# Interleaving two products, splitting the attend and moving fill pieces in a recurrent-memory step

## The chip, the cores and the metric

The kernel runs on one core of one Trainium2 chip. The metric is device time in microseconds (us) of one execution. Several executions of each kernel are taken, those of a comparison on one chip in the same rounds. The record marks every run quoted here as of the fast state; their mean granted TensorE clock is 0.971 to 0.995. A ratio of two kernels is the mean time of one kernel's fast runs over that of the other's of the same rounds, so it is not quite the ratio of the medians that are quoted beside it.

## The reference, cut to what matters

The output is a gated mix of two branches. Branch B is an ordinary gated feed-forward layer and the change does not touch it. Branch A is a recurrence: 64 segments of 32 rows are done one after the other, and 8 memory rows of a segment's output are fed into the next.

```python
mem = mem0
for s in range(n_seg):                              # 64 steps, each needs mem of the one before
    h = concat([mem, x[32*s : 32*s+32]])            # 40 rows, 1024 wide
    q, k, v = h @ Wq, h @ Wk, h @ Wv                # 32 heads of 128
    p = softmax(mask(q @ k.T * scale))
    o = (p @ v) @ Wo
    mem = o[:8]                                     # to the next step
    outs.append(o[8:])
```

## The kernel before: the parts that matter

A step works on two halves of the heads, r = 0 and r = 1. TensorE runs 64 products in a fixed order, the "walk". A q, k or v product is 4 matmuls of 512 columns that run side by side in the array; an o product is 8 matmuls of 256 columns.

```python
ORDER = (("k", 0), ("q", 0), ("v", 0), ("k", 1), ("q", 1), ("o", 0), ("v", 1), ("o", 1))
walk = [(m, r, i) for m, r in ORDER for i in seq(m, r)]      # 8 products each
```

I call the eight groups k0, q0, v0, k1, q1, o0, v1, o1. The weights do not all fit into SBUF. Twelve slots of 512 KB are "paired": k 0 and 2, q 0 and 2, v 0, 1, 2, 4, 6, o 0, 2, 4. Such a slot is used first for one half and must be refetched from HBM before the other half's product of the same number. In half 0 the paired products come first, in half 1 last, so that a refetch has the longest time.

```python
def spent(k):                    # after a product
    n = home[k]
    done[n] += 1
    if done[n] < len(uses[n]) and uses[n][done[n]] != k:
        fetch(n)                 # 512 KB, issued on the SP queue when TensorE is done with the slot
```

Beside its own products a step has "fill pieces" f1 and f2, eight each: products for the row blocks that do not depend on the recurrence (f2 is a q fill in 29 of the 64 steps and a v fill in 30). They are placed where TensorE would otherwise wait for another engine.

```python
on("v", 0, 4, lambda: trans(qT))
on("q", 1, 4, lambda: trans(kT))
...
on("o", 0, 0, some(f1, 4))              # 4 pieces, while tA, tB of half 0 are made
on("o", 0, 0, lambda: attend(ua))       # p @ v: 16 matmuls with tA, vA, then 4 with tB, vB
on("o", 0, 0, some(f1, 1)); trans(qT); some(f1)         # (shortened)
on("o", 0, 1, lambda: scores(1))
...
on("o", 1, 0, lambda: evac(bank_of["v", 1], vA))        # ScalarE copies v1 to vA
on("o", 1, 0, some(f2, 5))
on("o", 1, 0, lambda: attend(ub))
on("o", 1, 0, some(f2))                 # the other 3
on("o", 1, 1, lambda: fill_evac(...))
...
# end of the step:
act_copy(a_bf, PB[XO])                  # two halves
if k2 and k2[0] == "q":
    fill_trans()                        # 4 transposes, in the gap while ScalarE copies a_bf
transpose(a_bf); dve_copy(h_next)       # the recurrence goes on with k0 of the next step
```

Matmuls of the attend use the array in four row tiles (a profile shows 32*128), products in four column tiles (128*32), transposes the whole (128*128). And one detail of memory turns out to matter: `vA = al("vA", [128, 4, 128], at=oT.off)`, that is, vA lies in the memory of oT, which the o products read.

## Time and profile before

| | before |
|---|---|
| time, median of 3 (lowest to highest) | 2300.04 us (2299.81 to 2300.23) |
| one recurrent step, mean of 62 | 24.50 us |
| TensorE busy | 89% |
| refetched weights | 12 of 512 KB a step, 513 MB in q1 over the whole run, start-up and feed-forward included |

These are lines of the page of the kernel before: the span, TensorE (PE) busy time, two costly groups, and two DMA queues with packets, megabytes and the share of 16 DMA engines. A group line has source line, engine, operation, out<-in, count, busy us and mean ns, then idle us before it.

```profile
span 2304.5 us, 80168 instructions
PE 2060.9 (89%) x36594; PEld 1099.2 (48%) x36614; DVE 901.2 (39%) x2164; ACT 604.1 (26%) x1280; POOL 616.0 (27%) x1107
...
L670 PE MATMUL pb<-sl,hT 128*32 128x512 bf16 x12288 | 756.8, 383 | 43.2 <-DMA sl<-in_A_Wq_dram 18.4
...
L682 PE MATMUL pb<-sl,oT 128*32 128x256 bf16 x8192 | 281.8, 275 | 56.2 <-issue 46.1
...
q1 hardware_dynamic: 189536, 513.35, 61.7%
...
q8 instruction: 287, 4.70, 0.8%
```

What TensorE waits for in the recurrent part is in the waits view (matmuls only, 150 to 1690 us; who waited, for whom, total us, times, longest):

```profile
PE pb L682 <- issue: 46.1, 44, 2.3
PE pb L670 <- DMA sl<-in_A_Wq_dram: 18.4, 28, 1.6
...
PE pb L670 <- issue: 8.5, 12, 1.4
PE pb L670 <- DMA sl<-in_A_Wv_dram: 7.9, 13, 1.0
...
PE pb L682 <- DMA sl<-in_A_Wo_dram: 7.6, 14, 1.0
```

L682 are the o products, L670 the q, k and v products. "Issue" means that no semaphore ended the gap. Looked at one by one, these gaps end about 2.4 us (median of 81; half of them between 2.33 and 2.48) after a 16,384-byte packet of the instruction queue (q8) started, so I read them as TensorE having no instructions to run. The Trainium skill, "Runtime: NRT & Kernel Launch", Instruction fetch mechanics, says that instructions are refilled by DMA in 16 KiB blocks of 256 and calls the cost of crossing a block "mostly hidden". The block size agrees (287 packets, 4.70 MB); hidden it is not here.

The end of a step, from the timeline of TensorE (start, length, engine, line, operation; L697 are fill pieces, L641 and L646 the two parts of the attend, L588 transposes, L871 the transposes of a_bf):

```profile
1014.03 1.25 PE L697 MATMUL pb<-sl,hR 128*32 128x512 bf16 x20
1015.21 0.27 PE L641 MATMUL pb<-tA,vA 32*128 32x40 bf16 x16
1015.33 0.19 PE L646 MATMUL pb<-tB,vB 32*128 32x64 bf16 x4
1015.45 0.83 PE L697 MATMUL pb<-sl,hR 128*32 128x512 bf16 x12
...
1018.63 0.40 PE L588 MATMUL pb<-ident,tok 128*128 128x128 bf16 x4
1019.08 0.40 PE L871 MATMUL pb<-ident,a_bf 128*128 128x128 bf16 x2
1019.58 2.77 PE L670 MATMUL pb<-sl,hT 128*32 128x512 bf16 x48
```

The reader sees five pieces (x20), the attend in one go, three pieces (x12); at the end the q fill's transposes fill the gap before the a_bf transposes. In a step with a v fill nothing stands there, and TensorE is idle for some 0.4 us.

### The profile page before, as it was taken

Reading aid. Unit: us, or ns where it says so; the run is one execution under the profiler, and the core shown is the slowest. Engines: PE = TensorE matmul, PEld = TensorE weight load, DVE = VectorE, ACT = ScalarE, POOL = GpSimd, SP = SyncE. Lnnn points to the kernel's source line nnn. Section 1 sums busy time; section 2 is a strip of 40 time slices with the busy share of each in tenths; the row PEclk is TensorE's granted clock in tenths of the full one; section 3 lists DMA queues with packets and bytes.
Section 4 is the critical chain, followed back from the end, with each engine's and each line's share of the span. In section 5 each row is a group of like instructions: output and inputs, shape, how many; then the busy total and the mean of one; then the engine's idle time right before and its main releaser. Section 6 shows DMA issues by size and latency. Waiting matters only on the chain.

```text
span 2304.5 us, 80168 instructions
## 1 busy us (share of the span) xinstructions
PE 2060.9 (89%) x36594; PEld 1099.2 (48%) x36614; DVE 901.2 (39%) x2164; ACT 604.1 (26%) x1280; POOL 616.0 (27%) x1107
## 2 busy tenths in 40 slices
PE   2588998899999998898998998998879999999998
PEld 1244555555555555555555455554444444444443
DVE  3134333334334343343343433333335164363452
ACT  1122232222323222232232322222223032131230
POOL 5233333343333433333333333333210000000000
PEclk9999999999999999999999999999999999999999
DMA  9968788788788787787887887887782802606206
GB/s 358 379 213 305 257 304 294 261 289 309 265 303 302 272 316 271 269 322 265 290 323 248 302 302 256 302 303 266 270 330 90 276 34 80 230 1 208 103 1 237
DMA packets 225714, 576.45 MB, mean 250 GB/s; under 512 B 30424, under 2 KB 42584, under 8 KB 225376
## 3 DMA queue, kind: packets, MB, share of 16 engines
q1 hardware_dynamic: 189536, 513.35, 61.7%
q0 software_dynamic: 26624, 44.14, 5.6%
q10 hardware_dynamic: 9216, 13.83, 1.7%
q8 instruction: 287, 4.70, 0.8%
q14 instruction: 51, 0.42, 0.1%
HBM read 539.71 MB, written 31.39 MB: 248 GB/s over the span
## 4 chain that ended last, share of the span: by engine, by line
PE 65%; DMA 24%; issue 5%; DVE 3%; ACT 2%; POOL 1%; SPq 0%; ACTq 0%; POOLq 0%; DVEq 0%
PE pb L670 20%; PE pb L929 14%; DMA sl<-in_A_Wq_dram 11%; PE pb L682 9%; PE pb L697 6%; PE pb L966 6%; DMA sl<-in_A_Wo_dram 5%; PE pb L712 3%; PE pb L588 3%; DMA sl<-in_A_Wv_dram 3%; DMA wd<-in_B_w_down_dram 2%; PE pb L609 1%; DMA xr_scr<-xr 1%; PE pb L641 1%; PE pb L603 1%
## 5 line engine op out<-in xcount | busy, mean ns | idle before, releaser
L670 PE MATMUL pb<-sl,hT 128*32 128x512 bf16 x12288 | 756.8, 383 | 43.2 <-DMA sl<-in_A_Wq_dram 18.4
L670 PEld LDWEIGHTS pb<-sl,hT 128*32 128x32 bf16 x12288 | 331.7, 97 | 327.2 <-DMA sl<-in_A_Wq_dram 38.8
L682 PE MATMUL pb<-sl,oT 128*32 128x256 bf16 x8192 | 281.8, 275 | 56.2 <-issue 46.1
L576 ACT ACTIVATE tok<-pb 128x512 bf16<-128x512 f32 x320 | 191.0, 597 | 458.0 <-PE pb L670 393.0
L682 PEld LDWEIGHTS pb<-sl,oT 128*32 128x32 bf16 x8192 | 213.0, 97 | 98.7 <-issue 54.6
L697 PE MATMUL pb<-sl,hR 128*32 128x512 bf16 x3072 | 215.0, 390 | 19.6 <-DMA sl<-in_A_Wq_dram 7.3
L929 PE MATMUL pb<-xT,wg 128*128 128x512 bf16 x896 | 213.2, 381 | 16.2 <-DVE GT L945 8.4
L655 POOL COPY oRc<-oT 128x128 bf16<-128x128 bf16 x128 | 98.6, 770 | 452.4 <-DVE oT L579 445.4
L929 PE MATMUL pb<-xT,wu 128*128 128x512 bf16 x896 | 211.7, 379 | 0.0
L966 PE MATMUL pb<-wd,GT 128*128 128x512 bf16 x876 | 194.7, 379 | 8.9 <-DMA wd<-in_B_w_down_dram 7.7
L579 DVE CAST oT<-pb 128x160 bf16<-128x160 f32 x256 | 71.2, 320 | 230.4 <-PE pb L646 230.4
L937 ACT ACTIVATE s<-pb 128x512 f32<-128x512 f32 x112 | 66.8, 596 | 326.8 <-PE pb L929 307.3
L929 PEld LDWEIGHTS pb<-xT,wg 128*128 128x128 bf16 x896 | 87.1, 98 | 125.1 <-DVE GT L945 12.8
L576 ACT ACTIVATE vA<-pb 128x512 bf16<-128x512 f32 x128 | 76.4, 597 | 265.9 <-PE pb L670 265.9
L966 PEld LDWEIGHTS pb<-wd,GT 128*128 128x128 bf16 x896 | 86.4, 98 | 117.2 <-DMA wd<-in_B_w_down_dram 15.5
L588 PE MATMUL pb<-ident,tok 128*128 128x128 bf16 x1280 | 128.1, 222 | 13.2 <-ACT tok L576 8.9
L929 PEld LDWEIGHTS pb<-xT,wu 128*128 128x128 bf16 x896 | 87.7, 98 | 105.9 <-issue 0.3
L938 DVE SCALAR_TENSOR_TENSOR tp<-s,pb 128x512 f32<-128x512 f32 x112 | 76.9, 687 | 155.2 <-ACT s L937 155.1
L588 PEld LDWEIGHTS pb<-ident,tok 128*128 128x128 bf16 x1280 | 72.6, 98 | 123.2 <-ACT tok L576 94.3
L579 DVE COPY kT<-pb 128x512 bf16<-128x512 bf16 x128 | 51.9, 405 | 197.9 <-PE pb L588 197.9
L614 DVE TENSOR_REDUCE st<-pb 128x8 f32<-128x320 f32 x128 | 62.9, 492 | 159.6 <-PE pb L609 159.6
L697 PEld LDWEIGHTS pb<-sl,hR 128*32 128x32 bf16 x3072 | 83.3, 98 | 81.5 <-DMA sl<-in_A_Wq_dram 8.4
(76 smaller groups left out, 1929.7 us busy)
## 6 DMA issues: line engine op xcount, KB each, us to landing
sl<-in_A_Wv_dram SPq DMA_DIRECT2D x331, 512.0 KB, 9.9
sl<-in_A_Wo_dram SPq DMA_DIRECT2D x205, 512.0 KB, 5.9
sl<-in_A_Wk_dram SPq DMA_DIRECT2D x142, 512.0 KB, 5.5
sl<-in_A_Wq_dram SPq DMA_DIRECT2D x142, 512.0 KB, 7.4
wd<-in_B_w_down_dram SPq DMA_DIRECT2D x56, 1024.0 KB, 6.4
qk_scr<-stg POOLq DMA_DIRECT2D x64, 128.0 KB, 5.8
qkr<-qk_scr POOLq DMA_DIRECT2D x128, 64.0 KB, 5.4
wg<-in_B_w_gate_dram SPq DMA_DIRECT2D x3, 1792.0 KB, 13.2
```

The lines of the kernel that those rows point to most:

```text
L576: op("act", lambda e: e.activation(o, i, ACTF.Copy), rd=rd, wr=wr)
L579: op("dve", lambda e: e.tensor_copy(o, i), rd=rd, wr=wr)
L588: ins = e.transpose(PBV[TT][:, j * 128:(j + 1) * 128], tok[:, j * 128:(j + 1) * 128], ident[:, :])
L655: op("pool", lambda e: e.tensor_copy(oRc[:, u, :, :].rearrange("p c x -> p x c"), oT[:, :, :, 32:40].rearrange("p g j c -> p (g j) c")), r ...
L670: ins = e.matmul(PB[bk][32 * g:32 * g + 32, :], lhsT=h[:, i, :], rhs=w[:, g * 512:(g + 1) * 512], start=(p % 8 == 0), stop=(p % 8 == 7))
L682: ins = e.matmul(PB[XO][32 * g:32 * g + 32, 0:256], lhsT=oT[:, gp_, 2 * jj + hh, 0:32], rhs=w[:, c:c + 256], start=(r == 0 and p % 8 == 0 ...
L697: ins = e.matmul(PB[b][32 * g:32 * g + 32, :], lhsT=h[:, k[2], :], rhs=w[:, g * 512:(g + 1) * 512], start=(n == 0), stop=(n == 7))
L712: ins = e.matmul(PB[b][32 * g:32 * g + 32, 0:256], lhsT=t[:, :, 2 * i + hh], rhs=w[:, c:c + 256], start=(ends[0] and i == 0 and hh == 0), ...
L929: ins = e.matmul(PB[bk][:, 0:FB], lhsT=w[:, kc, cc:cc + 128], rhs=xT[:, :, :, kc, :].rearrange("p t i c -> p (t i) c"), start=(kc == 0), s ...
L937: op("act", lambda e, hg=hg: e.activation(s1[:, :], hg, ACTF.Square, scale=SQ), rd=[BK(bg)], wr=[s1.r()])
L938: op("dve", lambda e, hg=hg, t=t: e.scalar_tensor_tensor(out=t[:, :], in0=s1[:, :], scalar=1.0, in1=hg, op0=ALU.add, op1=ALU.mult), rd=[BK ...
L966: ins = e.matmul(PB[bank[2 * k + hf]][:, :], lhsT=GT[:, j, tb * 128:(tb + 1) * 128], rhs=w[:, jj, hf * 512:(hf + 1) * 512], start=(j == 0) ...
```

## The change

Its intent: finish v1 two products earlier, so that its copy to vA is ready sooner; let the main part of the attend go as soon as tA is there and the small tail with tB a little later; with fewer pieces needed before and after the attend, put the two pieces saved into the gap at the end of the step, for every kind of f2 fill. The transposes of a q fill, which stood in that gap, go into the next step's k0.

```diff
-        walk = [(m, r, i) for m, r in ORDER for i in seq(m, r)]
+        groups = [[(m, r, i, n) for n, i in enumerate(seq(m, r))] for m, r in ORDER]
+        walk = [x for g in groups[:5] for x in g] + [groups[5 + (c == "v")].pop(0) for c in "ooovvovvovvovvoo"] + groups[7]
 # ... in scores(): pA and tA are now made before pB and tB; E8 lies 128 bytes later, clear of tA ...
 # ... attend() is split: attend() has the 16 matmuls of tA and vA, attend_tail() the 4 of tB and vB ...
-            on("v", 0, 4, lambda: trans(qT))
+            on("v", 0, 5, lambda: trans(qT))
-            on("q", 1, 4, lambda: trans(kT))
+            on("q", 1, 5, lambda: trans(kT))
-            on("o", 0, 0, some(f1, 4))
+            on("o", 0, 0, some(f1, 2))
             on("o", 0, 0, lambda: attend(ua))
+            on("o", 0, 0, some(f1, 2))
+            on("o", 0, 0, lambda: attend_tail(ua))
-            on("o", 1, 0, some(f2, 5))
+            on("o", 1, 0, some(f2, 3))
             on("o", 1, 0, lambda: attend(ub))
-            on("o", 1, 0, some(f2))
-            if k2:
-                on("o", 1, 1, lambda: fill_evac(*k2, F2, stage[1]))
+            on("o", 1, 0, some(f2, 1))
+            on("o", 1, 0, lambda: attend_tail(ub))
+            on("o", 1, 0, some(f2, 2))
 # ... end of the step, after the copies to a_bf:
-            if k2 and k2[0] == "q":
-                fill_trans()
+            run(f2)                                   # the last two pieces
+            if k2:
+                fill_evac(*k2, F2, stage[1])
 # ... after the copies to h_next:
             if k2 and k2[0] == "q":
-                fill_put(stage[1], "dve")
+                pend.append(fill_trans)               # run at product 4 of the next k0
+                pend.append(lambda: fill_put(stage[1], "dve"))
```

## The prediction

> **What bounds the kernel.** TensorE is busy 89% of 2304.5 us (engine table). The change touches the 64 recurrent steps (about 120 to 1680 us), 24.5 us each by the transpose that starts a step (timeline). Of these I count, from starts of matmuls against the usual spacing of the same pair, 21.7 us of undisturbed issue and some 2.3 us of stalls:
> - About 1.2 us "issue": no semaphore ends these gaps. They end 2.2 to 2.5 us after a 16 KB packet of the instruction queue starts, so I read them as TensorE waiting for instructions. Some 0.9 us of it lies in o0 and early v1, where products of 8 matmuls of 256 columns use instructions fastest. The Trainium skill ("Runtime: NRT & Kernel Launch", Instruction fetch mechanics) has blocks of 256 instructions fetched by DMA, "mostly hidden"; the trace agrees on the block (287 packets of 16,384 bytes), not on "hidden".
> - About 0.8 us weight DMA (waits view, weight loads in the phase: Wq 38.8, Wv 17.1, Wo 13.1 us). The 12 refetches of a step land every 1.3 to 1.7 us from 5.6 to 22.6 us of the step; the last Wv lands at 18.15 (used at 18.98), the last Wo at 22.56 (used at 23.47). So a step can shrink by 0.5 to 0.7 us at most, some 40 us in all.
> - 650 ns from the last o matmul to the a_bf transpose, in steps without a waiting q fill.
>
> **What the change does, per step.**
> 1. Two fill pieces (217 ns each) into the 650 ns gap. In the 30 steps with a v fill this is free: -0.43 us. In the 30 with a q fill, the fill transposes sat there; they move into the next step's k0, where such a set costs 312 + 168 + 149 - 217 = 0.41 us: net zero, part hidden in the Wq wait.
> 2. Attend split: one more switch between row-tiled and column-tiled matmuls. Product to attend takes 312 ns against 217, attend to product 114; one more round costs 312 + 114 - 217 - 14 = 0.195 us, 0.39 us a step. ("TensorEngine Tiling (Array Packing)", Key Properties: mode switches drain the array; 312 against 217 agrees.)
> 3. Attend hardly waited for tA, tB or vA (matmul idle 7 us in all), so "waits on tA only" gains nothing itself; it lets pieces move. With two pieces instead of three after the o1 attend, the first o1 product waits about 0.13 us for oT.
> 4. Interleaving lowers the instruction rate: o0 used 16 instructions per 0.24 us, the mix 24 per 0.46. I guess 0.35 of the 0.9 us goes. But v1's last refetched pair is used 0.48 us earlier, against 0.8 us of median slack: Wv and Wo waits grow by 0.17.
> 5. Transposes one product later: the 311 ns before them is the drain, so nothing is gained.
>
> Sum: v steps -0.43 +0.39 +0.13 -0.35 +0.17 = -0.1 us; q steps up to +0.3, half absorbed. I add 5 us for chances of better instruction timing and predict **2291 us**, 2268 to 2314; faster by over 2%: 0.07, within 2%: 0.89, slower: 0.04.
>
> **Right if** fill matmuls fill the gap before the a_bf transpose; each attend shows two 312 ns entries; "issue" before Wo products falls by a third; waits for Wv rise; Wq waits fall after q fills; steps average 24.3 to 24.6 us.
>
> **Wrong if** the instruction stalls depend on where blocks of 256 fall (every reorder shifts them), which can swing 1 us a step; if Wv/Wo waits eat more than 0.2; or if fill stores, now 1.5 us later, ease or crowd the first refetches (the first takes 4.6 us, later ones land every 1.5).

## The result, and the profile after

| | before | after |
|---|---|---|
| median (lowest to highest), 4 runs each | 2300.14 us (2299.81 to 2310.69) | 2324.74 us (2322.47 to 2332.34) |
| ratio, 95% interval | | 1.0102 (1.0065 to 1.0138) |
| one recurrent step in the profiled run, mean of 62 | 24.50 us | 24.73 us |

The kernel became 1% slower, and the time lies outside the range predicted. The two profiled runs are 19.2 us apart (2304.5 and 2323.7); 14 us of that lie in 62 steps (62 times 0.226), the rest before and after.

The page and the waits of the kernel after (L690 are now the o products, L679 the q, k and v products):

```profile
span 2323.7 us, 80137 instructions
PE 2094.9 (90%) x36614; PEld 1095.0 (47%) x36614; DVE 914.4 (39%) x2164; ACT 604.9 (26%) x1280; POOL 613.7 (26%) x1107
...
PE pb L690 <- issue: 36.6, 38, 2.1
PE pb L679 <- DMA sl<-in_A_Wv_dram: 24.5, 33, 2.0
PE pb L679 <- issue: 11.0, 10, 2.5
PE pb L679 <- DMA sl<-in_A_Wq_dram: 10.9, 21, 1.1
```

Waits for instructions at the o products fell by 9.5 us (and rose by 2.5 at the others), those for Wq fell by 7.5, and those for Wv went from 7.9 to 24.5. The timeline of one step's second half shows all parts of the change (L705 fill pieces, L645 and L655 the two parts of the attend, L881 a_bf):

```profile
1003.65 0.40 PE L679 MATMUL pb<-sl,hT 128*32 128x512 bf16 x4
1004.95 0.40 PE L679 MATMUL pb<-sl,hT 128*32 128x512 bf16 x4 [0.90 <-DMA sl<-in_A_Wv_dram]
...
1006.06 0.82 PE L705 MATMUL pb<-sl,hR 128*32 128x512 bf16 x12
1006.94 0.27 PE L645 MATMUL pb<-tA,vA 32*128 32x40 bf16 x16
1007.14 0.40 PE L705 MATMUL pb<-sl,hR 128*32 128x512 bf16 x4
1007.47 0.21 PE L655 MATMUL pb<-tB,vB 32*128 32x64 bf16 x4
1007.61 0.61 PE L705 MATMUL pb<-sl,hR 128*32 128x512 bf16 x8
...
1009.84 0.61 PE L705 MATMUL pb<-sl,hR 128*32 128x512 bf16 x8
1010.40 0.40 PE L881 MATMUL pb<-ident,a_bf 128*128 128x128 bf16 x2
1010.90 1.05 PE L679 MATMUL pb<-sl,hT 128*32 128x512 bf16 x16
1011.88 0.40 PE L591 MATMUL pb<-ident,tok 128*128 128x128 bf16 x4
1012.21 2.13 PE L679 MATMUL pb<-sl,hT 128*32 128x512 bf16 x36
```

The last refetched v product waits 0.90 us for its weights. The tail starts 0.33 us after the single piece (a piece alone takes 0.217). Two pieces (x8) fill the gap before L881 as meant, and the q fill's transposes (L591) now interrupt k0, at 1011.88.

The second attend also waited for vA. Its copy should have started earlier than before; it did not. These are the groups of ScalarE's waits before its copies to vA, first of the kernel before, then of the kernel after:

```profile
ACT vA L576 <- PE pb L670: 265.9, 127, 5.8
```

```profile
ACT vA L579 <- PE pb L690: 101.2, 34, 4.8
ACT vA L579 <- PE pb L679: 99.1, 63, 1.6
```

Before, all copies waited for the v products. After, 34 of the 64 copies of v1 waited for the o products (L690): vA lies in the memory of oT, so the copy may not start before the last o product has read it, and that is now the last of the mixed group. In 28 steps ScalarE also had a stage copy to do just before, whose place (at o product 6) had moved behind most of v1:

```profile
1005.72 0.60 ACT L579 ACTIVATE stg<-pb 128x512 bf16<-128x512 bf16 x1 [2.92 <-PE pb L591]
1006.28 0.60 ACT L579 ACTIVATE vA<-pb 128x512 bf16<-128x512 f32 x1
```

The stage copy is not what held it: in all 62 steps looked at, with or without it, the copy to vA starts 36 to 53 ns after the last o0 product ended (before: 36 to 52 ns after the last v1 product). So the head start that v1's earlier end was to give did not exist. The second attend starts 54 to 57 ns after the copy's end in every one of these steps.

### The profile page after: what moved, and what is told of

Its sections match the earlier page's. It is cut to its first block, busy times and chain, and to the rows that moved or that the text cites. A ratio compares the mean times of both kernels' runs of the same rounds, so it can differ in the third digit from the quotient of the medians.

```text
span 2323.7 us, 80137 instructions
## 1 busy us (share of the span) xinstructions
PE 2094.9 (90%) x36614; PEld 1095.0 (47%) x36614; DVE 914.4 (39%) x2164; ACT 604.9 (26%) x1280; POOL 613.7 (26%) x1107
## 4 chain that ended last, share of the span: by engine, by line
PE 63%; DMA 27%; issue 4%; DVE 3%; ACT 2%; POOL 1%; SPq 0%; ACTq 0%; POOLq 0%; DVEq 0%
PE pb L679 19%; DMA sl<-in_A_Wv_dram 15%; PE pb L940 14%; PE pb L690 8%; PE pb L977 6%; DMA sl<-in_A_Wq_dram 6%; PE pb L705 5%; PE pb L591 3%; PE pb L720 3%; DMA wd<-in_B_w_down_dram 2%; ACT vA L579 1%; DMA sl<-in_A_Wo_dram 1%; DMA xr_scr<-xr 1%; PE pb L645 1%; PE pb L612 1%
## 5 line engine op out<-in xcount | busy, mean ns | idle before, releaser
L679 PE MATMUL pb<-sl,hT 128*32 128x512 bf16 x12288 | 797.4, 381 | 56.3 <-DMA sl<-in_A_Wv_dram 25.1
L679 PEld LDWEIGHTS pb<-sl,hT 128*32 128x32 bf16 x12288 | 327.0, 96 | 307.5 <-DMA sl<-in_A_Wv_dram 40.5
L690 PE MATMUL pb<-sl,oT 128*32 128x256 bf16 x8192 | 331.2, 275 | 40.7 <-issue 36.6
L690 PEld LDWEIGHTS pb<-sl,oT 128*32 128x32 bf16 x8192 | 222.4, 97 | 122.3 <-issue 47.7
L705 PE MATMUL pb<-sl,hR 128*32 128x512 bf16 x3072 | 243.6, 395 | 19.9 <-DMA sl<-in_A_Wq_dram 8.9
L591 PE MATMUL pb<-ident,tok 128*128 128x128 bf16 x1280 | 127.8, 223 | 9.9 <-ACT tok L579 6.5
L591 PEld LDWEIGHTS pb<-ident,tok 128*128 128x128 bf16 x1280 | 72.7, 98 | 128.4 <-ACT tok L579 96.2
L953 DVE SCALAR_TENSOR_TENSOR tp<-tp,pb 128x512 f32<-128x512 f32 x112 | 76.9, 687 | 78.7 <-ACT tp L952 78.7
## 6 DMA issues: line engine op xcount, KB each, us to landing
wg<-in_B_w_gate_dram SPq DMA_DIRECT2D x3, 1792.0 KB, 14.3
```

Of the source, the lines that this page charges most:

```text
L591: ins = e.transpose(PBV[TT][:, j * 128:(j + 1) * 128], tok[:, j * 128:(j + 1) * 128], ident[:, :])
L679: ins = e.matmul(PB[bk][32 * g:32 * g + 32, :], lhsT=h[:, i, :], rhs=w[:, g * 512:(g + 1) * 512], start=(n == 0), stop=(n == 7))
L690: ins = e.matmul(PB[XO][32 * g:32 * g + 32, 0:256], lhsT=oT[:, gp_, 2 * jj + hh, 0:32], rhs=w[:, c:c + 256], start=(r == 0 and n == 0 and ...
L705: ins = e.matmul(PB[b][32 * g:32 * g + 32, :], lhsT=h[:, k[2], :], rhs=w[:, g * 512:(g + 1) * 512], start=(n == 0), stop=(n == 7))
L953: op("dve", lambda e, hu=hu, t=t: e.scalar_tensor_tensor(out=t[:, :], in0=t[:, :], scalar=1.0, in1=hu, op0=ALU.add, op1=ALU.mult), rd=[BK( ...
```

## The experiments

Theory A: TensorE itself got more work per step (two more switches between row and column tiles, q transposes out of the gap into k0, a wait for vA) than the filled gap gives back, and interleaving gives nothing, since what it could save in waits for instructions it loses in waits for Wv. Rivals: B, the interleaving does save instruction stalls, as predicted, and something else costs more; C, the whole loss is waits for refetched weights; D, interleaving costs TensorE time itself; and, for single parts, that the switches or the moved transposes are hidden in waits.

To judge, I use the mean time of a step's sections, taken from the starts of matmuls in the profiled run (62 steps), and a tally of TensorE's gaps: every gap of over 380 ns between the starts of two successive matmuls in these steps, except before the a_bf transpose, less 217 ns, put down to what released it (217 ns is the usual spacing of two products); "instructions" are gaps that no semaphore ended, within 3.6 us after an instruction packet started. Totals are in us over 62 steps:

| kernel | instructions | Wq | Wv | Wo | vA |
|---|---|---|---|---|---|
| before | 70.8 | 24.6 | 10.7 | 8.1 | 3.5 |
| after | 60.3 | 16.2 | 30.4 | 1.1 | 15.4 |
| e1 interleaving alone | 67.0 | 14.1 | 28.7 | 1.7 | 3.1 |
| e3 end pieces, v steps | 75.4 | 20.5 | 9.6 | 11.5 | 3.5 |
| e4 end pieces, all steps | 83.3 | 15.5 | 5.5 | 17.6 | 3.5 |
| e7 after, not interleaved | 69.3 | 22.0 | 6.4 | 9.6 | 15.6 |
| e8 other order | 78.7 | 21.5 | 5.8 | 3.6 | 3.5 |
| f1 before, no refetches | 0 | 0 | 0 | 0 | 3.4 |
| f2 after, no refetches | 0 | 0 | 0 | 0 | 15.2 |

These are of one profiled run each; differences of a few us between rows mean little. The vA column overstates the rise: a piece and the attend after it start 312 ns apart even without a wait, so each new vA gap counts 95 ns too much. Against these 312 ns the second attend of the kernel after starts 0.10 us a step later than in the kernel before, 6 us in all.

### Parts of the change alone

All are made from the kernel before, with that part only.

**e1: interleaving.**

```diff
-        walk: o0 then v1        (oooooooovvvvvvvv)
+        walk: o0 and v1 mixed   (ooovvovvovvovvoo)
```

> The kernel before with only the o0/v1 interleaving (ooovvovvovvovvoo). Theory A (the interleaving costs, because v1's refetched pairs are used 0.5 us earlier while their landing does not move): waits for Wv rise by 0.3 us a step or more, instruction stalls fall by only 0.15, Wo waits fall by 0.1: 0 to +8 us against before. Rival B (the interleaving saves instruction stalls as the prediction had it, and the loss lies in the split of attend and in the moved transposes): -10 to -20 us.

Measured: 2303.88 us against 2299.24, ratio 1.0021 (0.9992 to 1.0049), about +5 us, not clear of noise (in the profiled run a step takes 24.50 us, as before). It fits theory A; the 10 to 20 us gain of B lies outside the interval. The waits of e1 (L684 o products, L673 q, k and v):

```profile
PE pb L684 <- issue: 43.2, 42, 2.6
PE pb L673 <- DMA sl<-in_A_Wv_dram: 24.9, 38, 1.7
...
PE pb L673 <- issue: 12.0, 10, 2.4
PE pb L673 <- DMA sl<-in_A_Wq_dram: 9.1, 21, 1.4
```

Issue of both kinds is 55.2 against 54.6 before: nothing saved. Wv went from 7.9 to 24.9, and part of that came back from Wq and Wo. In the tally, Wv and Wo together went from 18.8 to 30.4, 0.19 us a step.

**e2: attend split**, with one piece between main part and tail, the number of pieces in each half unchanged.

```diff
-            some(f1, 4); attend(ua); some(f1, 1)
+            some(f1, 3); attend(ua); some(f1, 1); attend_tail(ua); some(f1, 1)
-            some(f2, 5); attend(ub); some(f2)
+            some(f2, 4); attend(ub); some(f2, 1); attend_tail(ub); some(f2)
```

> The kernel before with only attend split into a main part and a tail with one fill piece between them (same number of pieces in each half). Theory A and the prediction's step 2: two more drains a step, 0.195 us each, so +0.39 us a step on TensorE; where the step then waits less for weights, part is hidden: +12 to +25 us. Rival (drains are hidden, the split is free): within 3 us of before.

Measured: 2311.22 us, ratio 1.0043 (1.0014 to 1.0071), about +10 us, a little under the range that theory A gave. The split is not free. How much of its cost hides is shown by f4 below.

**e3: end pieces in v steps only** (4 pieces, attend, 2, and 2 at the end), attend whole.

```diff
-            some(f2, 5); attend(ub); some(f2)
+            some(f2, 4); attend(ub); some(f2, 2 if k2 and k2[0] == "v" else 99)
+            run(f2)                      # after the copies to a_bf
+            if k2 and k2[0] == "v":
+                fill_evac(*k2, F2, stage[1])
```

> The kernel before with two of the v fill's pieces moved behind the last o product, only in the 30 steps with a v fill (pieces 4 + attend + 2, then 2 at the end). Both theories: the gap before the a_bf transpose is filled for free, -0.43 us in 30 steps and +0.06 for a wait on oT: -11 us; if the weight DMA sets the pace of a step, Wo and Wq waits take much of it back and it is -3 us or less.

Measured: 2296.84 us, ratio 0.9983 (0.9952 to 1.0015), about -4 us, not clear of noise. Less than the 11 us of theory A, and in the direction of the limit named there: waits for Wo rose from 8.1 to 11.5 us and those for instructions from 70.8 to 75.4.

**e4: end pieces in all steps**, q transposes in the next k0, attend whole: the end part of the change.

```diff
-            if k2 and k2[0] == "q":
-                fill_trans()
+            run(f2)
+            if k2:
+                fill_evac(*k2, F2, stage[1])
+            # q: fill_trans and fill_put appended to pend, run at product 4 of the next k0
```

> As e3, and also in the 30 steps with a q fill, whose transposes then move into the next step's k0 as in the change. Prediction's step 1: the q steps gain 0.43 and the next k0 loses 0.41, so no better than e3 (-8 to -11 us). Rival (the moved transposes hide in the wait for Wq): another -8 to -12 us beyond e3.

Measured: 2308.02 us, ratio 1.0036 (0.9998 to 1.0074), about +8 us, just not clear of noise, and outside what either theory gave: 12 us worse than e3. From the start of k0 to the scores, steps after a q fill take 6.63 us at the median against 6.18 before, about what was predicted for the transposes; but the gain in the q steps is not seen, and waits for Wo are 17.6 us against 8.1.

**e10: the q transposes moved into k0, and nothing put into the gap.**

```diff
-            if k2 and k2[0] == "q":
-                fill_trans()
-                fill_put(stage[1], "dve")
+                pend.append(fill_trans)
+                pend.append(lambda: fill_put(stage[1], "dve"))
```

> The kernel before with only the q fill's transposes moved from the end of the step into the next step's k0 (nothing put in their place). Theory A: the gap they leave stays about 650 ns, the k0 part of the following step grows by 0.41 us in 30 steps: +8 to +12 us. The prediction's 'half absorbed' by the wait for Wq: +3 to +6 us. If the Wq wait hides all of it: 0.

Measured: 2317.14 us against 2303.17, ratio 1.0056 (1.0018 to 1.0094), about +13 us. That is all of the 29 sets (0.44 us each in f2 below, 12.9 us; the prediction had 0.41); half of it hiding in the Wq wait, as predicted, is not seen in the time, though the Wq wait did fall to 14.3 us from 24.6 in the tally. The runs of this kernel spread from 2304.83 to 2331.75, so the size is good to a few us only.

The parts alone add up: e1 +5, e2 +10 and e4 +8 make +23 us; the change as a whole costs 24 us. Each part is good to some 7 to 9 us, so the close match is partly luck. Without refetches the same three parts give 0, +27 and -8 us (f3, f4 and f6 below).

### Undoing the interleaving

**e7: the kernel after with o0 and v1 in their old order.**

```diff
-        ... for c in "ooovvovvovvovvoo"]
+        ... for c in "oooooooovvvvvvvv"]
```

> The changed kernel with o0 and v1 in their old order, all else changed. From e1 (+5 us alone): undoing the interleaving gives back about 5 us, +17 to +20 us against before; but v1 then ends right before the second attend with only 3 fill pieces to cover the copy to vA, which costs up to 0.4 us a step, so +25 to +45 us if that wait is not hidden. Rival B (interleaving saves stalls): well over +24 us without any longer wait for vA.

Measured: 2329.01 us against 2304.06, ratio 1.0109 (1.0094 to 1.0124), about +25 us, the same as the change itself within the noise (1.0109 against 1.0102). Waits for Wv fell from 30.4 to 6.4 us, and those for instructions, Wq and Wo rose by 9.0, 5.8 and 8.5: they come in each other's place. (The mixed order has 9.0 us less of instruction waits here, more than the 3.8 in e1, and no shorter time.) The wait for vA is 15.6 us with the old order and 15.4 with the new one. So my expectation that the mixed order shortens that wait was wrong, and it agrees with what was read above: the copy to vA starts after the last of the 16 products of o0 and v1, which is an o0 product in the mixed order and a v1 product in the old one (here 37 to 52 ns after its end).

### The same mixing with the refetched pairs later

**e8: another mixed order.**

```diff
-        walk: o0 then v1        (oooooooovvvvvvvv)
+        walk: o0 and v1 mixed   (ooovovovovovovvv)
```

> The kernel before with o0 and v1 interleaved in another order (ooovovovovovovvv): the same mixing, but v1's last three refetched pairs stay in their old places. Theory A (the refetched pairs' earlier use is what made e1 lose): Wv waits back at 0.2 us a step, instruction stalls still 0.1 to 0.2 below before: -3 to -10 us, some 10 us better than e1. Rival D (the interleaving itself costs, wherever the pairs lie): no better than e1, +3 us or more.

Measured: 2300.12 us against 2304.06, ratio 0.9978 (0.9963 to 0.9992), about -5 us, a small gain that is clear of noise, and 10 us better than e1. The waits of e8, same lines as for e1:

```profile
PE pb L684 <- issue: 52.9, 51, 2.3
PE pb L673 <- DMA sl<-in_A_Wq_dram: 15.5, 30, 1.5
...
PE pb L673 <- issue: 10.1, 10, 2.1
PE pb L673 <- DMA sl<-in_A_Wv_dram: 4.0, 9, 0.8
```

Wv is back at 4.0 us, so the earlier use of the pairs is what raised it in e1. But my expectation had the gain come from fewer instruction stalls, and issue is not lower at all (63.0 for the two lines, against 54.6 before). Put into the kernel before, mixing the products does not clearly relieve TensorE of waits for instructions in either order. Why e8 is 5 us faster these lines leave open, beyond lower waits for Wv, Wq and Wo together (30.9 in the tally, 43.4 before).

### Without refetches

These kernels keep each paired slot's first weights and never refetch them. TensorE runs the same matmuls; the results are wrong. (The comparison with the reference does not tell right weights from wrong ones here.) The edit is one line:

```diff
-            if done[n] < len(uses[n]) and uses[n][done[n]] != k:
+            if done[n] < len(uses[n]) and uses[n][done[n]] != k and k[0] not in ('k', 'q', 'v', 'o'):
```

**f1 is the kernel before without refetches.**

> The kernel before without any of the 12 refetches of a step (paired slots keep their first weights, so the result is wrong on purpose; TensorE does the same matmuls). Every theory: the waits for weights (about 0.8 us a step) are gone, -40 to -50 us. If the 2.2 to 2.5 us from an instruction packet to the end of a stall is the load of the DMA engines, the instruction stalls (about 1.2 us a step) mostly go as well, and it is -90 to -130 us; if that latency is its own, only the first part goes.

**f2 is the kernel after without refetches.**

> The changed kernel, also without refetches (wrong result on purpose). Against f1, theory A (TensorE pays for the split 0.39 us a step and for the moved transposes 0.2, gets 0.40 back in the end gap, and loses about 0.1 waiting for vA and oT; the interleaving has nothing to give without stalls): +12 to +20 us. Rival C (the whole loss is waits for refetched weights): within 4 us of f1.

Measured: f1 2149.06 us (ratio to before 0.9326), f2 2173.13 us (0.9437). f1 is 155 us faster than before, more than every estimate of its expectation. The profiled steps shrink by 143 us, of which the columns of the tally hold 114. I did not look into the rest. Its page and the longest waits:

```profile
span 2149.0 us, 79403 instructions
...
q1 hardware_dynamic: 54368, 110.65, 14.3%
...
PE pb L872 <- ACT a_bf L579: 13.1, 34, 0.4
PE pb L930 <- DMA wg<-in_B_w_gate_dram: 8.0, 1, 8.0
PE pb L644 <- ACT vA L579: 3.5, 5, 0.7
```

No wait for "issue" is left in this list, and none in the tally. The instruction packets are as many (287) and take as long (1.06 us at the median, 1.01 before), yet TensorE never waits for them. Counting the instructions that TensorE had started when each packet began, less 256 for each packet, the median packet of the recurrent part begins some 150 instructions after the earliest one's place in the kernel before and some 50 in f1. So with the refetches the packets begin later; the stalls come with the refetch traffic. That they stand behind weight packets there is my reading; the trace does not show when a packet was asked for.

f2 is 24 us slower than f1, with no weight waits and no instruction waits at all. That rejects rival C, and it is what theory A says, a little over its range. (That this equals the loss with refetches is partly luck: there the profiled steps grew by only 14 us, so some 10 of the 24 did not show in them, where the waits for instructions and weights in the tally are 6 us shorter; the rest of the loss lay outside these steps.) Where the 24 us lie is plain, because without refetches nearly every section repeats to some 5 ns from one step to the fourth after it (the fills go round in four steps). The means of 62 steps:

| section, us | f1 | f2 | difference |
|---|---|---|---|
| start of k0 to first scores | 6.182 | 6.390 | +0.208 |
| first scores to first attend | 5.298 | 4.893 | -0.405 |
| first attend to first o0 product | 1.574 | 2.206 | +0.632 |
| second scores to second attend | 5.101 | 4.807 | -0.294 |
| second attend to its last matmul | 0.126 | 0.519 | +0.393 |
| from there to the first o1 product | 0.762 | 0.609 | -0.153 |
| rest, from o1 to the next k0 and o0 to second scores | 3.143 | 3.152 | +0.009 |
| step | 22.186 | 22.575 | +0.389 |

62 times 0.389 are 24.1 us, the difference of the medians. The first line is the q transposes (0.444 us after each of 29 q fills). From the start of the last o product's last matmul to the a_bf transpose it is 0.657 us in both: the pieces at the end are free.

**f3: e1 without refetches.** The edits are those of e1 and f1.

> e1 without refetches (wrong result on purpose). Theory A (interleaving moves only waits, TensorE itself takes as long): within 2 us of f1, 2149 us. Rival D (switching between o and v products costs TensorE time): +5 us or more.

Measured: 2147.31 us, ratio to before 0.9324 against 0.9326 of f1. All sections agree with f1 to 2 ns. Rival D is out: interleaving costs and saves TensorE nothing.

**f4: e2 without refetches.**

> e2 without refetches (wrong result on purpose). Theory A: with no waits to hide in, the split costs its full two drains a step, 0.39 to 0.41 us in 62 steps: +24 us against f1 (2149 us), where e2 with refetches cost 10 us. If the split itself were cheaper than the prediction had it: +10 us here too.

Measured: 2177.71 us, ratio 0.9453. A step takes 22.618 us, 0.432 more than f1: 0.226 in the first half and 0.206 in the second. 62 times that are 27 us. So the split costs its full price and a little more than predicted; with refetches it showed as 10 us, because TensorE then waited less for weights.

After these runs it was open why the end pieces gave so little in e3 and e4.

**f5 and f6: e3 and e4 without refetches.**

> e3 without refetches (wrong result on purpose). Theory A (filling the end gap saves TensorE its full 0.43 us less 0.06 for oT in 30 steps, and in e3 later waits for instructions and for Wo took two thirds back): -9 to -11 us against f1 (0.9326 of before), so about 0.928 to 0.929 of before. Rival E (the pieces are not free at the end, TensorE itself saves only the 4 us of e3): 0.931.

> e4 without refetches (wrong result on purpose). Theory A: the 30 q steps gain the same 0.37 us as the v steps and their following steps lose 0.41 us for the moved transposes, so +1 us against f5. Rival F (in q steps the gap fill saves nothing even on TensorE): as e4 stood against e3, +12 us against f5.

Measured: f5 2141.77 us (ratio 0.9290), f6 2138.74 us (0.9285). A step takes 22.012 us in f5 and 22.057 in f6, against 22.186 in f1. The v steps gain 0.37 us in f5, exactly what theory A had; in f6 the q steps gain the same and lose 0.44 in the next k0. (The medians of f5 and f6 lie the other way round; that difference is outside the 62 steps.) Rivals E and F are out: TensorE does save this time. With refetches e3 and e4 show less of it. The five columns of the tally together rise by 3 us in e3 and by 8 in e4, so TensorE gives part of it back in waits for weights and instructions; that this is all is not shown.

### The best of the parts

**e9: the order of e8 and the end pieces of e3.**

> The two parts that gained alone, together: the order of e8 and the end pieces of e3 in v steps only; attend unsplit, transposes where they were. If they add, -4 and -5 us: -9 us against before. If both live off the same slack before the last Wo and Wv land, no better than -5 us.

Measured: 2294.85 us against 2303.17, ratio 0.9974 (0.9940 to 1.0009), about -6 us. That is faster than the changed kernel by far, and the best median against its own rounds of all kernels with right results, but not clear of the kernel before. The two gains do not add to 9 us clearly.

## Why the prediction was wrong, point by point

It said 2291 us, 2268 to 2314; measured were 2324.74.

- **What bounds the kernel**: right in kind. Waits for instructions and for refetched weights are the stalls. It treated the two as separate; f1 shows that both go when the refetches go.
- **Step 1, end pieces and q transposes**: the sizes were right on TensorE (0.37 us net per v step in f5, 0.44 per moved set in f6, where 0.41 was predicted). "Part hidden in the Wq wait" and "half absorbed" failed: e10 cost 13 us where half would be 6. And in the v steps the gain came to about 4 us where the sum had 11.
- **Step 2, the split**: right: 0.39 predicted, 0.43 measured without refetches (f4). "TensorEngine Tiling (Array Packing)", Key Properties, says a change of mode drains the array; the 312 ns against 217 agrees.
- **Step 3, vA and oT**: "attend hardly waited" was read from the kernel before and taken over to the kernel after, where only three pieces stand before the second attend. There the wait for vA is 15.4 us in the tally against 3.5. In the sums of f2 it is what is left over: 0.389 less f4's 0.432 and f6's -0.129 is 0.086 us a step, 5 us, close to the 0.10 us read from the spacing in the kernel after. I had overlooked that vA lies in oT's memory. The wait for oT was over-estimated (0.064 us against 0.13, from 0.609 less 0.762 plus one piece of 0.217).
- **Step 4, interleaving: this is the step that failed.** "I guess 0.35 of the 0.9 us goes" stood for 22 us over the phase. In e1 the tally has 67.0 us of instruction stalls against 70.8, 0.06 us a step; in the whole change, 60.3, 0.17 us a step, half of the guess, and undoing the mixing there (e7) cost no time. The step took the rate at which TensorE uses instructions for what sets these stalls. What the runs show in its place is the refetch traffic: with the same order of products and no refetches they are 0 (f1), and mixing then changes nothing (f3). The other half of that step, waits for Wv and Wo up by 0.17 us a step, was right (0.19).
- **Step 5, transposes one product later**: not tried alone. Weight loads of transposes waited 81.9 us for tok before and 82.1 after in the same window, so nothing was gained by it.
- The extra 5 us "for chances of better instruction timing" had no ground at all. Nor do the terms give 2291: -0.09 us in 30 v steps and half of +0.3 in as many q steps are about +2 us in all, which less the 5 is 2297. Some 6 us of the forecast stand on no term.
- **Its own signs**: the pieces fill the gap, Wv waits rise and Wq waits fall, as it said. "Issue" before the o products fell by a fifth (46.1 to 36.6), not by a third, and the step of 24.73 us lies outside 24.3 to 24.6.

Taken together: 18 us from the interleaving guess (22 less 4), 6 to 7 from the absorption that did not happen, 5 from the chance bonus, 5 from vA and 6 that stood on no term, less 4 for oT, are about 37 us above 2291; measured were 34. With the fall of 10.5 us in instruction stalls that the whole change shows, the first term is 11 and the sum 30. It is a rough sum, since with refetches the parts hide behind each other.

What stays open: why a lower instruction rate reduced the stalls for instructions so little, and what exactly an instruction packet waits for before it begins.

## What to carry to other kernels

Price a reordering with all memory waits taken away first: here the wrong-result kernels without refetches showed to a few ns what each part costs TensorE, which the loaded kernel blurs by giving back gains and hiding losses in other waits. The split let part of a group go earlier although the group was hardly waiting, and so it only added a switch of tile mode. And before moving a producer earlier to give its copy a head start, look at what shares the memory of the copy's target and what else the copying engine has to do then.

## What the Trainium skill lacked or had wrong

- "Runtime: NRT & Kernel Launch", Instruction fetch mechanics: the cost of crossing a block is called mostly hidden. In the kernel before TensorE waited 70.8 us in 62 steps for instructions (81 gaps), with weights streaming by DMA at the same time; without the refetches it waited 0, with as many packets. The page does not say that the fetch depends on other DMA load.
- The same page gives PE 2048 instructions of buffer. In the kernel before at most 145 instructions ran between the start of the last instruction packet and the end of a stall (74 gaps of over 450 ns between weight loads or matmuls); so the packet that TensorE then waited for had begun less than one block of 256 ahead. That says how far ahead the fetch ran under load; the size of the buffer was not measured.
- "TensorEngine Tiling (Array Packing)", Key Properties: says that a change of mode drains the array, but gives no duration. Here one more round from column tiles to row tiles and back cost 0.206 to 0.226 us (f4 less f1), beside products of 512 columns; a whole-array set of four transposes in a row of such products cost 0.444 us (f2 less f1).
